# Two transformer layers on one core: implied dependencies declared away in the attention, output weights in a pool on the other side, chunk 1's operands in place of the exponentials

## The chip, the cores and the metric

The kernel runs on one core of a Trainium2 chip. The metric is the device time of one execution in microseconds (us). The engines are named as in the profile: PE (TensorE, matmuls), PEld (its weight loads), DVE (VectorE), ACT (ScalarE), POOL (GpSimd) and SP (SyncE, which here issues nearly all DMAs). Each works through its own instructions in order, and waits on semaphores that others raise.

## The reference

Two identical layers on `x` of 2048 rows by 448 columns, in float32. Each is a grouped attention with one key and one value head for 16 query heads of 28, and a gated feed-forward of width 1792, both behind a layer norm and with a residual sum:

```python
def _A_ref(x, wq, wk, wv, wo):
    q = (x @ wq).reshape(B, S, H, Dh).transpose(0, 2, 1, 3)
    k = x @ wk
    v = x @ wv
    scores = jnp.einsum("bhqd,bkd->bhqk", q, k) * (Dh ** -0.5)
    p = _softmax(scores, axis=-1)
    o = jnp.einsum("bhqk,bkd->bhqd", p, v)
    return o.transpose(0, 2, 1, 3).reshape(B, S, H * Dh) @ wo

def _B_ref(x, w_gate, w_up, w_down):
    return (_silu(x @ w_gate) * (x @ w_up)) @ w_down

x = x + _A_ref(_layernorm(x), wq, wk, wv, wo)
x = x + _B_ref(_layernorm(x), w_gate, w_up, w_down)
# and both once more
```

## The kernel before, in words

The order of instructions on each engine is the order in which the program issues them; no scheduler moves them. Semaphore waits are put in by the framework from the tiles that instructions read and write. Where an instruction needs more than one wait, wait instructions of their own stand ahead of it on its queue. A tile pool that is opened where another was closed reuses its memory, and each tile waits for the readers and writers of what lay there (`reuse_waits="tile"`).

**Precision.** Matmul operands are split into a high and a low part, so that a product of `a` and `b` is three matmuls (high by high, high by low, low by high). The 2048 rows of `x` are worked in four *chunks* of 512, whose transposed operands are a pair of tiles, `xh` and `xl`. The 448 columns are four row blocks of which the last is half full; it holds the high and the low part in one block, and a tile `xd` has those rows once more on the other half of the partitions.

**The attention's loop (`Attention.scores`).** Queries are taken in 16 groups (a chunk by four heads), keys in 16 tiles of 128. A *cycle* `m` takes two key tiles of a group, so there are 8 cycles a group and 128 a layer. In one cycle

- PE computes the scores of the first key tile for four heads (`tile_scores`, line 590): three heads go to a triple bank of PSUM, `three`, and the fourth to a single bank. Then those of the second key tile, to the other triple bank and the other single bank. The two single banks change roles from cycle to cycle.
- ACT computes four exponentials: the first single bank (line 607), the first triple (608), the second triple (611), and the second single (612). The second single was copied out of PSUM by DVE (line 610) before.
- PE multiplies the exponentials of the cycle *before* by the values (`pv`, line 639) into the single bank whose exponential line 607 has just read.
- DVE adds this product to the group's sum (line 648, or 646 for a group's first cycle). The scores of the next second key tile go to that bank, so they wait for this sum.

The exponentials have four buffers of each size, `pt` (three heads) and `pt1` (one head). After the last cycle of a group `post` sends row sums through DRAM, and a few cycles later multiplies by their reciprocals and splits the result into `onh` and `onl`. When a chunk is complete, its output projection (`outproj`, lines 575 and 579, with the weights `woh` and `wol`) stands between two cycles, three times a layer. Norm and transposition of finished chunks are dealt out over later cycles; they reach the feed-forward through DRAM (`ff.raw`).

Ahead of the loop, `q` computes queries, keys and values; ACT copies each result to a staging tile (`stage`, line 524), and SP stores it to DRAM (lines 525 and 528). `key_load` (line 383) reads the last chunk's keys back.

**The seam.** After the last cycle the feed-forward's first two units (`ff.unit(0, 0, 0)` and `(0, 0, 1)`) are issued, then the output projection of the last chunk, then `ff.rest`. A *unit* is one block of 128 of the 1792 hidden columns for one chunk: gate and up products in two halves of 11 and 10 pairs of matmuls (line 318; the two of a pair use the upper and the lower half of the array), with the down product of the unit before between and behind them. Chunk 0's operands were made during the attention. Those of chunk 1 (`parts(1, ...)`: line 278 copies on ACT, line 279 subtracts on DVE, lines 285 to 288 for the last block) are made at the start of `rest`; those of chunk 2 on POOL by the same lines, after the unit `(0, 1, 0)`; chunk 3's norm (lines 217 to 232) and transposition follow. Lines 809 and 810 add part of each chunk's down product to the residual, by a staging tile that ACT writes and POOL reads.

The pool `at` of the attention holds `woh`, `wol`, the exponentials, `tb`, `onh`, `onl` and small tiles. It is closed after the last output projection, and `stage`, `xb` (three pairs of operands) and `xd` are opened in its place.

Of the kernel before, what the change touches and what calls it, by code (L numbers as in the profile page):

```python
# [15 lines left out]
P = 128  # L16
# [39 lines left out]
def forward(  # L56
# [272 lines left out]
    class Attention:  # L329
# [223 lines left out]

        def scores(self, ff):
            next(switch)
            with tc.tile_pool(name=f"at{self.layer}", bufs=1, reuse_waits="tile") as wp:
                woh = wp.tile([P, NG, D], F32R, name="woh")
                wol = wp.tile([P, NG, D], F32R, name="wol")
                on, accs, pts = {}, {}, {}
# [23 lines left out]
                def tile_scores(n, three, one):  # L583
# [3 lines left out]
                    for z, (kp, part) in enumerate(((0, 0), (1, 0), (0, 1))):  # L587
                        for j in range(4):
# [4 lines left out]
                            )  # L593
                    pt = wp.tile([P, 3, 512], F32, name="pt", bufs=4)
                    pt1 = wp.tile([P, 512], F32, name="pt1", bufs=4)
                    pts[n] = [*(pt[:, j, :] for j in range(3)), pt1]
                    return pt, pt1

                def singles(m):
# [3 lines left out]
                def cycle(m):  # L603

                    a, b = singles(m)
                    pt, pt1 = tile_scores(2 * m, threes[0], a)
                    nc.scalar.activation(pt1, a, AF.Exp, scale=SCALE)
                    nc.scalar.activation(pt, threes[0], AF.Exp, scale=SCALE)  # L608
                    pt, pt1 = tile_scores(2 * m + 1, threes[1], b)
                    nc.vector.tensor_copy(pt1, b)  # L610
                    nc.scalar.activation(pt, threes[1], AF.Exp, scale=SCALE)  # L611
                    nc.scalar.activation(pt1, pt1, AF.Exp, scale=SCALE)

# [19 lines left out]
                def pv(m, to):  # L633
# [10 lines left out]
                    if u == 0:  # L644
                        accs[i] = halves("o2").bitcast(F32)
                        nc.vector.tensor_copy(accs[i][:, 0, :], to)
                    else:
                        nc.vector.tensor_tensor(accs[i][:, 0, :], to, accs[i][:, 0, :], ALU.add)  # L648
                    if u == NT // 2 - 1:
                        due[m + 3] = post(i)  # L650

                def post(i):
# [3 lines left out]
                    oraw, rb = out2[:, 0, :], out2[:, 1, :]  # L656
                    rs = wp.tile([P, 16], F32, name="rs", bufs=2)
                    for j in range(4):
                        nc.sync.dma_start(rs[32 * j : 32 * j + 32, :], oraw[32 * j + DH : 32 * j + DH + 1, :])

                    def rest():
                        if fine is not None:
                            under = wp.tile([P, 16], F32, name="under", bufs=2)
                            for bound, op in ((LIMIT, ALU.is_lt), (1.0 / LIMIT, ALU.is_gt)):
                                nc.vector.tensor_scalar(under, rs, bound, None, op)
                                nc.vector.tensor_tensor(fine, fine, under, ALU.mult)
# [4 lines left out]
                        if g == 0:  # L671
                            on[c] = (
                                wp.tile([P, NG, 512], F32R, name="onh"),
                                wp.tile([P, NG, 512], F32R, name="onl"),
                            )
# [68 lines left out]
                pv(last - 1, banks[6])  # L744
                self.lent = None
                next(switch)
                ff.X[0] = X0
                ff.unit(0, 0, 0)
                due.popitem()[1]()
                ff.unit(0, 0, 1)  # L750
                pos = [bank(LOW)[1] for _ in range(4)]
# [10 lines left out]
    class FeedForward:  # L762
# [61 lines left out]
        def hand_over(self, c):  # L824
# [5 lines left out]
            a.pool = self.stage  # L830
            a.X[c] = xtile(xpool if c == 0 else self.xbp)

# [91 lines left out]
        def verdict(self, last):  # L924
# [6 lines left out]
            nc.vector.tensor_reduce(whole, row[0:1, 0:P], AX.X, ALU.min)  # L931

        def rest(self, xb):
            self.stage = xb.enter_context(tc.tile_pool(name=f"stage{self.layer}", bufs=2, reuse_waits="tile"))
            self.xbp = xb.enter_context(tc.tile_pool(name=f"xb{self.layer + 1}", bufs=3, reuse_waits="tile"))
            xd = xb.enter_context(tc.tile_pool(name=f"xd{self.layer}", bufs=1, reuse_waits="tile"))
            self.xd = [xd.tile([P, 512], F32R, name=f"xd{c}") for c in range(NC)]
            dma(self.xd[0][64:128, :], self.X[0][0][0:64, 3, :])
            self.X[0] = (*self.X[0][:2], self.xd[0])
            self.parts(1, nc.scalar.copy, nc.vector.tensor_tensor)  # L940
            fs3, self.norms[3] = norm_steps(3)
            for f in fs3[:5]:
                f()
            self.fetch(2)
            self.soon.append([0, lambda: self.parts(2, nc.gpsimd.tensor_copy, nc.gpsimd.tensor_tensor)])
            self.soon.append([1, lambda: [f() for f in fs3[5:]]])
# [63 lines left out]
    for layer in range(2):  # L1010
        at.finish()
        xb.close()
        ff = FeedForward(layer)
        at.scores(ff)
        xb = ExitStack()
        ff.rest(xb)
        at = ff.nxt
# [28 lines left out]
```

## Time and profile before

| | us |
|---|---|
| median of three runs | 1998.7 (1998.66, 1998.7, 2002.25) |
| the profiled execution | 2002.23 |
| its span, first to last instruction | 2000.5 |
| PE busy | 1978.4 |
| ACT busy | 1277.5 |
| DVE busy | 785.4 |
| POOL busy | 560.4 |

The attention of layer 0 lasts from about 64 to 571 on the trace's clock, that of layer 1 from about 1054 to 1561; the rest is projections and feed-forward. Lines of a timeline read: start, duration, engine, line, operation, output and inputs, and how many were merged. A bracket has the idle time of the engine before it, and what ended it. Ends of matmuls are modelled. ACTq and PEq are the sequencers of these engines, where wait instructions run. A row that follows a stretch has its length, the busy time of PE, PEld, DVE, ACT and POOL with the number of instructions, the granted clock of PE, the share of DMA, and GB/s.

### The profile page before, as it was taken

What the parts mean: (1) busy time and instruction counts of PE and PEld (TensorE: products, weight loads), DVE (VectorE), ACT (ScalarE), POOL (GpSimd) and SP (SyncE); (2) the same over time, 40 slices, a digit from 0 to 9 for tenths busy, and PEclk for the clock granted to TensorE, in tenths of its full rate; (3) what the DMA queues carried; (4) which work ended last, traced back from release to release, by engine and by line L of the source; (5) the groups of instructions that cost most, each with busy time, mean ns of one, the idle gap of its engine ahead of it and who ended that gap; (6) DMA issues with size and microseconds to landing.
All of it is one profiled execution on the core that took longest, in us unless ns stands there. A gap on an engine that the chain in (4) does not pass through costs nothing.

```text
span 2000.5 us, 44597 instructions
## 1 busy us (share of the span) xinstructions
PE 1978.4 (99%) x18517; PEld 1337.5 (67%) x18517; DVE 785.4 (39%) x1370; ACT 1277.5 (64%) x2142; POOL 560.4 (28%) x611
## 2 busy tenths in 40 slices
PE   9999999999999999999999999999999999999998
PEld 7544545445468999999884444454454789988887
DVE  6444443443543222322464334535444332222322
ACT  4899797997953333333349998979979433333332
POOL 5222213122214233333351221122221233233320
PEclk9999999999999999999999999999999999999999
DMA  5101020021211011110031010200212100011102
GB/s 164 52 24 37 12 57 17 22 51 32 44 42 35 25 32 31 32 31 22 12 100 35 25 31 12 62 13 26 52 37 58 45 16 22 26 31 32 32 1 76
DMA packets 126343, 75.30 MB, mean 38 GB/s; under 512 B 69656, under 2 KB 109976, under 8 KB 126136
## 3 DMA queue, kind: packets, MB, share of 16 engines
q1 hardware_dynamic: 124584, 71.20, 12.9%
q8 instruction: 146, 2.39, 0.5%
q10 hardware_dynamic: 1552, 1.20, 0.2%
q14 instruction: 61, 0.50, 0.1%
HBM read 54.01 MB, written 17.83 MB: 36 GB/s over the span
## 4 chain that ended last, share of the span: by engine, by line
PE 94%; DVE 2%; POOL 1%; ACT 1%; DMA 1%; issue 0%; ACTq 0%; POOLq 0%; SPq 0%; DVEq 0%
PE bank L318 39%; PE bank L639 24%; PE three L590 17%; PE bank L590 6%; PE bank L298 4%; PE three L575 2%; PE bank L575 2%; PE bank L248 1%; POOL xl L279 0%; DMA qd<-stage 0%; ACT pt L611 0%; DVE xn L230 0%; DMA xn<-xt 0%; DMA xres<-in_A_x_dram 0%; DVE xres L579 0%
## 5 line engine op out<-in xcount | busy, mean ns | idle before, releaser
L639 PE MATMUL bank<-pt,vsb 128*32 128x512 f32 x4096 | 493.2, 598 | 0.5
L590 PE MATMUL bank<-qstack,keys 32*128 32x512 f32 x1536 | 483.8, 424 | 1.7 <-DVE xres L579 1.7
L590 PE MATMUL three<-qstack,keys 32*128 32x512 f32 x4608 | 448.8, 420 | 1.4 <-ACT stage L524 1.0
L318 PE MATMUL bank<-xh,wgh 64*128 64x512 f32 x1728 | 443.7, 391 | 4.0 <-ACT xh L278 1.4
L590 PEld LDWEIGHTS three<-qstack,keys 32*128 32x128 f32 x4608 | 258.1, 182 | 282.2 <-ACT pt L608 185.2
L611 ACT ACTIVATE pt<-three 128x1536 f32<-128x1536 f32 x256 | 383.1, 1496 | 0.0
L608 ACT ACTIVATE pt<-three 128x1536 f32<-128x1536 f32 x256 | 379.4, 1482 | 0.0
L318 PE MATMUL bank<-xh,wgl 64*128 64x512 f32 x1404 | 366.2, 391 | 0.0
L318 PE MATMUL bank<-wdh,h 64*128 64x448 f32 x1792 | 333.1, 365 | 1.2 <-ACT h L904 0.8
L318 PE MATMUL bank<-xl,wgh 64*128 64x512 f32 x1296 | 331.4, 391 | 2.6 <-POOL xl L279 2.1
L903 DVE TENSOR_TENSOR sg<-bank,sg 128x512 f32<-128x512 f32 x112 | 77.5, 692 | 511.8 <-ACT sg L902 502.6
L318 PEld LDWEIGHTS bank<-xh,wgh 64*128 64x128 f32 x1728 | 261.2, 185 | 22.5 <-POOL xh L288 2.2
L639 PEld LDWEIGHTS bank<-pt,vsb 128*32 128x32 f32 x4096 | 107.1, 109 | 249.1 <-issue 152.6
L810 POOL TENSOR_TENSOR xres<-stage,xres 128x448 f32<-128x448 f32 x108 | 127.9, 1204 | 506.0 <-ACT stage L809 506.0
L648 DVE TENSOR_TENSOR o<-bank,o 128x512 f32<-128x512 f32 x224 | 155.0, 692 | 280.5 <-PE bank L639 276.4
L610 DVE COPY pt<-bank 128x512 f32<-128x512 f32 x256 | 176.9, 691 | 205.5 <-PE bank L590 203.1
L318 PEld LDWEIGHTS bank<-wdh,h 64*128 64x128 f32 x1792 | 244.3, 185 | 14.7 <-issue 2.3
L590 PEld LDWEIGHTS bank<-qstack,keys 32*128 32x128 f32 x1536 | 243.9, 183 | 7.8 <-DVE xres L579 3.6
L677 POOL TENSOR_TENSOR o<-o 128x512 f32<-128x512 f32 x32 | 41.2, 1289 | 739.7 <-DMA o<-rd 431.6
L325 ACT COPY seen<-bank 128x1 f32<-128x1 f32 x664 | 81.4, 163 | 255.0 <-PE bank L318 249.8
L318 PEld LDWEIGHTS bank<-xh,wgl 64*128 64x128 f32 x1404 | 214.7, 185 | 13.1
L318 PE MATMUL bank<-wdl,h 64*128 64x448 f32 x896 | 218.2, 368 | 0.0
(130 smaller groups left out, 2323.5 us busy)
## 6 DMA issues: line engine op xcount, KB each, us to landing
o<-rd SPq DMA_DIRECT2D x32, 256.0 KB
qd<-stage SPq DMA_DIRECT2D x32, 224.0 KB
qraw<-qd SPq DMA_DIRECT2D x128, 56.0 KB
wdr<-in_B_w_down_dram SPq DMA_DIRECT2D x28, 224.0 KB
xt<-tb SPq DMA_DIRECT2D x96, 56.0 KB
wr<-in_B_w_gate_dram SPq DMA_DIRECT2D x28, 192.0 KB
wr<-in_B_w_up_dram SPq DMA_DIRECT2D x28, 192.0 KB
xn<-xt SPq DMA_DIRECT2D x6, 768.0 KB
```

Source lines behind the costliest of these rows:

```text
L298: nc.tensor.matmul(po, a, b, start=(i == 0), stop=(i == len(seq) - 1))
L318: nc.tensor.matmul(po, a, b, start=start, stop=stop, skip_group_check=True)
L325: nc.scalar.copy(seen[:, i : i + 1], po[:, 0:1])
L575: nc.tensor.matmul(po[:, 0:D], a[:, g, ts_], b[:, g, :], start=(g + z == 0), stop=(g == NG - 1 and z == 2))
L590: nc.tensor.matmul(three[:, j, :] if j < 3 else one, k[js, kp, ks], q[js, part, :], start=(z == 0), stop=(z == 2), tile_position=(32 * j, 0),)
L608: nc.scalar.activation(pt, threes[0], AF.Exp, scale=SCALE)
L610: nc.vector.tensor_copy(pt1, b)
L611: nc.scalar.activation(pt, threes[1], AF.Exp, scale=SCALE)
L639: nc.tensor.matmul(to[32 * j : 32 * j + 32, :], vsb[:, n % NT, :], pts[n][j], start=(y == 0), stop=(y == 1), skip_group_check=True,)
L648: nc.vector.tensor_tensor(accs[i][:, 0, :], to, accs[i][:, 0, :], ALU.add)
L810: nc.gpsimd.tensor_tensor(r, s, r, ALU.add)
L903: nc.vector.tensor_tensor(sg, pg[1], sg, ALU.mult)
```

## The change

1. The pool `at` holds only the exponentials and `tb`. The output weights, `onh`, `onl` and the small tiles are in a new pool `ow` on the right side of the memory. `at` is closed right after the last P-V, before the feed-forward's first unit.
2. The exponentials have fixed buffers, taken in turn. Between an exponential and the one that wrote its buffer two cycles before, between the copy of line 610 and that exponential, and between DVE's sum and two of its partners (the sum before, and the exponential that freed its bank), the dependency is declared away, since another wait implies it.
3. Chunk 1's operands are made ahead of the unit `(0, 0, 0)`, by a new function `begin`, in a pool that takes the place of the exponentials. Their `xd` is filled by a DMA at the start of `rest`, as chunk 0's is. Chunk 2's load (`fetch(2)`) is issued between the first two units, and its parts are made on POOL at the start of `rest`.

```diff
-        def scores(self, ff):
+        def scores(self, ff, xb):
             next(switch)
-            with tc.tile_pool(name=f"at{self.layer}", bufs=1, reuse_waits="tile") as wp:
-                woh = wp.tile([P, NG, D], F32R, name="woh")
-                wol = wp.tile([P, NG, D], F32R, name="wol")
+            inner = ExitStack()
+            with tc.tile_pool(name=f"ow{self.layer}", bufs=1, side="right", reuse_waits="tile") as ow:
+                wp = inner.enter_context(tc.tile_pool(name=f"at{self.layer}", bufs=1, reuse_waits="tile"))
+                woh = ow.tile([P, NG, D], F32R, name="woh")
+                wol = ow.tile([P, NG, D], F32R, name="wol")
...
-                    pt = wp.tile([P, 3, 512], F32, name="pt", bufs=4)
-                    pt1 = wp.tile([P, 512], F32, name="pt1", bufs=4)
+                    pt, pt1 = bufs[n % 4]
...
+                exps, sums = {}, {}
+                bufs = [
+                    (wp.tile([P, 3, 512], F32, name=f"pt{y}"), wp.tile([P, 512], F32, name=f"single{y}"))
+                    for y in range(4)
+                ]
...
-                    nc.scalar.activation(pt1, a, AF.Exp, scale=SCALE)
-                    nc.scalar.activation(pt, threes[0], AF.Exp, scale=SCALE)
+                    es = [nc.scalar.activation(pt1, a, AF.Exp, scale=SCALE)]
+                    es.append(nc.scalar.activation(pt, threes[0], AF.Exp, scale=SCALE))
                     pt, pt1 = tile_scores(2 * m + 1, threes[1], b)
-                    nc.vector.tensor_copy(pt1, b)
-                    nc.scalar.activation(pt, threes[1], AF.Exp, scale=SCALE)
-                    nc.scalar.activation(pt1, pt1, AF.Exp, scale=SCALE)
+                    copy = nc.vector.tensor_copy(pt1, b)
+                    es.append(nc.scalar.activation(pt, threes[1], AF.Exp, scale=SCALE))
+                    es.append(nc.scalar.activation(pt1, pt1, AF.Exp, scale=SCALE))
+                    exps[m] = [e.ins for e in es]
+                    for new, old in zip(exps[m], exps.get(m - 2, ())):
+                        tc.declare_no_dep(new, old, reason="P-V, which read the buffer, waited for the old one")
+                    if m > 1:
+                        tc.declare_no_dep(copy.ins, exps[m - 2][3], reason="P-V, which read it, waited for that")
...
-                        nc.vector.tensor_copy(accs[i][:, 0, :], to)
+                        f = nc.vector.tensor_copy(accs[i][:, 0, :], to)
                     else:
-                        nc.vector.tensor_tensor(accs[i][:, 0, :], to, accs[i][:, 0, :], ALU.add)
+                        f = nc.vector.tensor_tensor(accs[i][:, 0, :], to, accs[i][:, 0, :], ALU.add)
+                        if m + 1 in exps:
+                            tc.declare_no_dep(f.ins, sums[m - 1], reason="scores, ahead of this P-V, waited for the sum")
+                    sums[m] = f.ins
+                    if m + 1 in exps:
+                        tc.declare_no_dep(f.ins, exps[m + 1][0], reason="P-V waited for the bank's exponential")
...
                 pv(last - 1, banks[6])
                 self.lent = None
+                inner.close()
                 next(switch)
                 ff.X[0] = X0
+                ff.begin(xb)
                 ff.unit(0, 0, 0)
                 due.popitem()[1]()
+                ff.fetch(2)
                 ff.unit(0, 0, 1)
...
-            a.X[c] = xtile(xpool if c == 0 else self.xbp)
+            a.X[c] = xtile((xpool, self.x1p, self.xbp, self.xbp)[c])
...
+        def begin(self, xb):
+
+            self.x1p = xb.enter_context(tc.tile_pool(name=f"x1{self.layer}", bufs=1, reuse_waits="tile"))
+            self.X[1] = xtile(self.x1p)
+            halved(self.X[1], self.got.pop(1), range(4), nc.scalar.copy, nc.vector.tensor_tensor)
+
         def rest(self, xb):
...
-            self.xbp = xb.enter_context(tc.tile_pool(name=f"xb{self.layer + 1}", bufs=3, reuse_waits="tile"))
+            self.xbp = xb.enter_context(tc.tile_pool(name=f"xb{self.layer + 1}", bufs=2, reuse_waits="tile"))
...
-            dma(self.xd[0][64:128, :], self.X[0][0][0:64, 3, :])
-            self.X[0] = (*self.X[0][:2], self.xd[0])
-            self.parts(1, nc.scalar.copy, nc.vector.tensor_tensor)
+            for c in range(2):
+                dma(self.xd[c][64:128, :], self.X[c][0][0:64, 3, :])
+                self.X[c] = (*self.X[c][:2], self.xd[c])
             fs3, self.norms[3] = norm_steps(3)
             for f in fs3[:5]:
                 f()
-            self.fetch(2)
-            self.soon.append([0, lambda: self.parts(2, nc.gpsimd.tensor_copy, nc.gpsimd.tensor_tensor)])
+            self.parts(2, nc.gpsimd.tensor_copy, nc.gpsimd.tensor_tensor)
...
-        at.scores(ff)
         xb = ExitStack()
+        at.scores(ff, xb)
         ff.rest(xb)
```

The other edits of the diff put `rs`, `under`, `onh` and `onl` into `ow`.

More of the change, by code (lines that the diff above doesn't have):

```diff
@@ L656, in post @@
                     oraw, rb = out2[:, 0, :], out2[:, 1, :]
-                    rs = wp.tile([P, 16], F32, name="rs", bufs=2)
+                    rs = ow.tile([P, 16], F32, name="rs", bufs=2)
                     for j in range(4):
@@ L662, in rest @@
                         if fine is not None:
-                            under = wp.tile([P, 16], F32, name="under", bufs=2)
+                            under = ow.tile([P, 16], F32, name="under", bufs=2)
                             for bound, op in ((LIMIT, ALU.is_lt), (1.0 / LIMIT, ALU.is_gt)):
@@ L672, in rest @@
                             on[c] = (
-                                wp.tile([P, NG, 512], F32R, name="onh"),
-                                wp.tile([P, NG, 512], F32R, name="onl"),
+                                ow.tile([P, NG, 512], F32R, name="onh"),
+                                ow.tile([P, NG, 512], F32R, name="onl"),
                             )
```

## The prediction

> **What bounds the kernel now.** I read the page first, then the timeline of each engine in the attention's loop, then the places where PE sits idle, at the seams between the stages.
>
> ```profile
> span 2000.5 us, 44597 instructions
> ...
> PE 1978.4 (99%) x18517; PEld 1337.5 (67%) x18517; DVE 785.4 (39%) x1370; ACT 1277.5 (64%) x2142; POOL 560.4 (28%) x611
> ...
> L611 ACT ACTIVATE pt<-three 128x1536 f32<-128x1536 f32 x256 | 383.1, 1496 | 0.0
> ```
>
> The 99% of PE looks like a verdict, and for the feed-forward stages it is one. In the attention it isn't: there ACT's large exponential has no idle time at all before it (the 0.0 of its group), so both engines look full, and the question is which chain closes the loop. A cycle is two key tiles: scores, four exponentials, and P-V of the cycle before. The rows of ACT's line 608 in one undisturbed stretch give its length: 31 starts, 30 steps from 216.4 to 327.1, so 3.69 us a cycle.
>
> ```profile
> L608 ACT ACTIVATE pt<-three x31: 1445/1462/1530, 216.4 to 327.1; 128x1536 f32<-128x1536 f32 x31
> ```
>
> What ACT alone would need shows where it starts, before P-V and its sums have come round (ACT's timeline):
>
> ```profile
> 65.51 1.47 ACT L608 ACTIVATE pt<-three 128x1536 f32<-128x1536 f32 x1
> 66.84 1.47 ACT L611 ACTIVATE pt<-three 128x1536 f32<-128x1536 f32 x1
> 68.18 0.66 ACT L612 ACTIVATE pt<-pt 128x512 f32<-128x512 f32 x1
> 68.69 0.63 ACT L607 ACTIVATE pt<-bank 128x512 f32<-128x512 f32 x1
> 69.17 1.49 ACT L608 ACTIVATE pt<-three 128x1536 f32<-128x1536 f32 x1
> ```
>
> From start to start that is 1.33 + 1.34 + 0.51 + 0.48 = 3.66. ACT is 0.03 short of its own floor in each steady cycle. What takes the 0.03 is seen when PE, PEld and DVE are laid beside each other, later in the same loop:
>
> ```profile
> 150.18 0.39 PE L590 MATMUL bank<-qstack,keys 32*128 32x512 f32 x1
> ...
> 150.50 1.92 PE L639 MATMUL bank<-pt,vsb 128*32 128x512 f32 x16
> 150.61 0.69 DVE L610 COPY pt<-bank 128x512 f32<-128x512 f32 x1 [1.06 <-PE bank L590]
> ...
> 152.55 0.69 DVE L648 TENSOR_TENSOR o<-bank,o 128x512 f32<-128x512 f32 x1 [1.25 <-PE bank L639]
> ...
> 153.30 0.18 PEld L590 LDWEIGHTS bank<-qstack,keys 32*128 32x128 f32 x1
> ...
> 154.18 1.92 PE L639 MATMUL bank<-pt,vsb 128*32 128x512 f32 x16
> ```
>
> P-V runs from 150.50 to 152.42; the sum (line 648) starts 0.13 later and ends at 153.24; 0.06 after that PE loads weights for the single bank that the sum has just read; 0.88 later, when those scores are through, the next P-V starts: 154.18, which is 3.68 after the last. That is a closed ring through PE and DVE, and it is longer than ACT's 3.66. So in the steady loop the ring of P-V, sum and scores is the bound, by 0.02 to 0.03, and ACT comes right behind it.
>
> **The change, part by part.**
>
> *Declared dependencies.* In the program as built, ACT loses the three wait instructions that stood in each cycle, and DVE's sum loses its one: what is left is a single wait, on PE, carried by the sum itself. The price on DVE can be read above. The copy of line 610 has one wait: its scores end at 150.18 + 0.39 = 150.57 and it starts 0.04 later. The sum has a wait instruction ahead of it: 0.13. So the ring gets 0.06 to 0.09 shorter (I leave 0.03 for ends that are modelled), to 3.59 to 3.62. That is below ACT's 3.66, so ACT becomes the bound, and only 0.03 a cycle can be had, whatever else the ring gives. There are 128 cycles a layer, three of which are stretched by the output projection of a chunk; of the 127 steps 124 are regular, 248 in both layers: 248 x 0.03 = **7.4 us**. What is late next is ACT itself. Its own wait instructions cost it nothing now:
>
> ```profile
> L611 ACTq EVENT_SEMAPHORE  x252: 17/17/17, 73.1 to 1557.3; - x126
> ```
>
> They take 17 ns on its queue while a 1.33 exponential runs; line 608, which has none, is followed after the same 1.33 as line 611, which has one. The bounds of this term: nothing, if the ring has a second branch as long; and 248 x 0.065 = 16, if ACT's floor came down with the waits too.
>
> *Output weights on the other side.* This moves addresses, and with them what a buffer has to wait for. The first buffer of exponentials now lies where the attention's three staging tiles were, and the exponential of line 608 in cycle 0 of layer 0 must wait until the last of them is stored. Two rows of SP's queue show when that is, because the load of line 383 waits for the same store:
>
> ```profile
> 65.72 0.39 SPq L528 DMA_DIRECT2D kt<-stage  x1
> ...
> 68.16 0.55 SPq L383 DMA_DIRECT2D wrk<-kt  x1
> ```
>
> Line 608 would start at 68.1 instead of 65.51, and as ACT is the bound from there on, nothing hides it: a **loss of 2.6 us**, once. In layer 1 the staging tiles lie under buffers that are needed a cycle later; I put that at nothing (bound: 0.5).
>
> *Chunk 1's operands in place of exponentials.* Four copies and four subtractions move from behind the last output projection to ahead of the first feed-forward unit, where ACT and DVE have time. The seam before:
>
> ```profile
> 592.28 2.46 DVE L579 TENSOR_TENSOR xres<-bank,xres 128x448 f32<-128x448 f32 x4 [1.47 <-PE bank L575]
> ...
> 593.71 0.37 PE L575 MATMUL bank<-woh,onl 128*128 128x448 f32 x1
> 593.95 0.54 SPq L127 DMA_DIRECT2D xd<-xh  x1
> 594.11 1.66 ACT L278 CAST xh<-xn 128x512 fp32r<-128x512 f32 x3 [4.02 <-PE bank L575]
> ...
> 594.78 0.50 PE L318 MATMUL bank<-xh,wgh 64*128 64x512 f32 x2 [0.71 <-ACT xh L278]
> ...
> 597.41 0.63 DVE L217 BATCH_NORM_STATS2 stats<-xres 128x6 f32<-128x448 f32 x1
> ...
> 602.69 0.46 PE L318 MATMUL bank<-xh,wgh 64*128 64x512 f32 x2
> 602.92 0.46 PE L318 MATMUL bank<-xl,wgh 64*128 64x512 f32 x2
> ...
> 609.98 0.46 PE L318 MATMUL bank<-xh,wgh 64*128 64x512 f32 x2
> ```
>
> An undisturbed unit takes 609.98 - 602.69 = 7.29. The one before it could have begun at 594.08 and took until 602.69: 8.61, so 1.3 too long. That goes. A new wait takes part of it back: chunk 1's extra rows (xd) are now a transfer, issued behind the one of chunk 0 on SP, and both wait for the last projection. Second in the queue it is issued at about 594.7, lands 2.4 later (the store above: 65.72 to 68.16) at 597.1, and PE wants it at the eleventh pair of matmuls, 10 x 0.23 after 594.08, at 596.4: 0.7 of stall, with the queue of PE behind it. Net 0.6 to 0.7 a layer, **1.3 us** in all; bounds 0 and 2.6.
>
> *Chunk 2 earlier.* The larger part of the seam is further on. Chunk 2's parts are made on POOL, and now stand ahead of two residual sums, with their load issued between the first two units, before the output projection:
>
> ```profile
> 600.52 0.20 POOL L222 TENSOR_SCALAR rstd<-mv 128x4 f32<-128x4 f32 x1 [11.09 <-DVE mv L218]
> 600.81 1.01 POOL L223 TENSOR_TENSOR rstd<-rstd,halfn 128x4 f32<-128x4 f32 x1
> 604.21 2.36 POOL L810 TENSOR_TENSOR xres<-stage,xres 128x448 f32<-128x448 f32 x2 [2.39 <-ACT stage L809]
> 606.52 0.61 POOL L278 CAST xh<-xn 128x512 fp32r<-128x512 f32 x1
> ...
> 614.26 1.26 POOL L288 TENSOR_TENSOR xh<-xn,xd 64x512 fp32r<-64x512 f32 x1
> ...
> 623.67 2.34 POOL L810 TENSOR_TENSOR xres<-stage,xres 128x448 f32<-128x448 f32 x2 [6.03 <-ACT stage L809]
> ```
>
> Line 222 waits for statistics on DVE, which begin at 597.41 today, after chunk 1's subtractions, and then right after line 579, at 594.74: 2.67 earlier. So lines 222 and 223 end at 599.15, and the parts, which take 615.52 - 606.52 = 9.0, at 608.2 instead of 615.5. Their unit starts at 609.98 now, 609.3 then. So its waits go:
>
> ```profile
> 612.90 0.50 PE L318 MATMUL bank<-xl,wgh 64*128 64x512 f32 x2 [1.07 <-POOL xl L279]
> ...
> 615.57 0.79 PE L318 MATMUL bank<-xh,wgh 64*128 64x512 f32 x1 [0.83 <-POOL xh L288]
> ...
> 609.98:622.00 12.02, 9.51 (x69) 7.78 (x67) 3.03 (x7) 1.99 (x8) 6.76 (x10) 0.86 0.01 3
> 1600.70:1613.90 13.20, 10.98 (x68) 8.72 (x66) 3.01 (x7) 1.99 (x8) 6.75 (x10) 0.74 0.00 0
> ```
>
> The last two rows are the same unit in both layers, from its start to the next one's. Against 7.29 it loses 4.7 and 5.9: **10.6 us**. The seventh number after the span is the granted clock, 0.86 and 0.74: PE ran at half speed for part of it, and that is why the layers differ. How much of the 10.6 is clock: the parts end at 615.52, and what is left of the unit after the first 11 pairs (7.29 - 2.53) would have it end at 620.3 instead of 622.00; 1.7, and 1.2 more in layer 1, so some 4. The two residual sums that are pushed back end at 610.5 instead of 606.6; ACT needs their staging tiles again for the sums at 623.67, ahead of which POOL idled 6.03, so that costs nothing (cover gone: 4).
>
> **The sum.** The profiled execution took 2002.23, its span is 2000.5. 2002.23 - 7.4 + 2.6 - 1.3 - 10.6 = 1985.5. Of the three timed runs one took 2002.25 and two 1998.7; the profiled one stands 3.5 above their median. I take these 3.5 to be about the clock's 4: then the runs at 1998.7 lose only 7.1 in that unit, and 1998.7 - 7.4 + 2.6 - 1.3 - 7.1 = 1985.5 as well. If the 3.5 lies elsewhere, it is 1982.0. A measurement here tells 0.2% (4 us) from no change.
>
> **The rivals.** *The waits cost nothing.* Wait instructions run ahead on their queue, and the ring is closed by something as long. For it: 17 ns on ACT. Against it: the 0.13 and 0.04 on DVE. The loop stays at 3.69: 1985.5 + 7.4 = 1992.9. [...]
>
> *ACT's floor falls too.* Each start of ACT may hold a fixed share for its waits. Against it: 1.33 with and without. The ring would then be the bound at about 3.625: 248 x 0.035 = 8.7 more, 1976.8.
>
> *Half clock stays.* The granted clock falls though the waits go: 3.5 of the gain is lost, 1989. For it: the waits of PE in that unit are 1.07 and less, and a clock that falls for another reason falls again. [...]
>
> *Slower: the exponentials' new places.* If ACT's writes and PE's reads of buffers that now alternate large and small get in each other's way, each of the 512 large exponentials pays. From 0.026 each (13.2 us) all gain is gone; at 0.05 it is 25.6 and 2011. Against it: today's four buffers lie apart, and all show 1.33.
>
> **How the numbers follow.** My forecast 0.60 (its own range 1981 to 1989: the start's and the transfer's bounds, and the 3.5); waits free 0.13; floor falls 0.10; half clock 0.09; slower 0.08. The range 1976.5 to 1994 leaves out the last and the far ends. Faster by over 0.2% (under 1994.7): 0.60 + 0.10 + 0.09 and 0.07 of the second, which with the other bounds at their worst is near no change; 0.86. Same: 0.06 of it and 0.01 of the slower case, 0.07. Slower 0.07.
>
> **What would show it.** Right: steps of 3.66 between line 608's starts (now 615) instead of 3.69, and the sum 0.05 or more closer to P-V's end; cycle 0's large exponential of layer 0 starting near 68; PE waiting under 1 for chunk 1's xd; chunk 2's unit 7.3 long, clock 1.00. Wrong: cycles still 3.69 (the ring isn't what I think), POOL's parts still ending after 611, or large exponentials further apart than 1.34.

## The result, and the profile after

| | us |
|---|---|
| before, median of 7 runs | 2000.29 (1998.66 to 2002.25) |
| after, median of 7 runs | 1992.85 (1990.6 to 1995.44) |
| ratio | 0.9961 (95%: 0.9951 to 0.9971) |
| the profiled execution after, and its span | 1995.44, 1993.7 |

The change makes the kernel 7.4 us faster. The time lies inside the forecast range, near its slow end of 1994, and 7.4 above the 1985.5 that was forecast. The page of the changed kernel, its span, its engines and the two groups that the prediction named (608 is now 615):

```profile
span 1993.7 us, 43630 instructions
...
PE 1973.1 (99%) x18517; PEld 1305.8 (65%) x18517; DVE 782.7 (39%) x1370; ACT 1276.1 (64%) x2140; POOL 559.9 (28%) x611
...
L618 ACT ACTIVATE pt<-three 128x1536 f32<-128x1536 f32 x256 | 408.7, 1597 | 0.0
L615 ACT ACTIVATE pt<-three 128x1536 f32<-128x1536 f32 x256 | 405.3, 1583 | 2.6 <-DMA kt<-stage 2.6
```

Two things stand out beside the shorter span. The same exponentials last longer, 1597 ns where line 611 had 1496. And line 615 has an idle time that 608 didn't have: 2.6, ended by the store of a staging tile (`stage`).

Where the time went is read by stage. The boundaries are starts in the timelines of ACT and PE: a layer's first exponential, the large exponential of cycle 2 and of cycle 127 (line 615 or 608), the last matmul of the last output projection, the first of line 318 behind it.

| stage | before | after | difference |
|---|---|---|---|
| to the first exponential, layer 0 | 65.02 | 68.09 | +3.07 |
| from there to cycle 2 | 7.80 | 11.91 | +4.11 |
| cycles 2 to 127 | 493.61 | 492.49 | -1.12 |
| to the end of the attention | 27.27 | 27.34 | +0.07 |
| from the last projection to the feed-forward | 1.08 | 0.30 | -0.78 |
| feed-forward, next layer's projections | 460.84 | 455.89 | -4.95 |
| layer 1: to cycle 2 | 7.81 | 8.33 | +0.52 |
| layer 1: cycles 2 to 127 | 493.70 | 492.12 | -1.58 |
| layer 1: to the end of the attention | 27.29 | 27.37 | +0.08 |
| layer 1: last projection to feed-forward | 1.07 | 0.30 | -0.77 |
| layer 1: feed-forward to PE's last matmul | 408.22 | 402.54 | -5.68 |

The seams give 12.2 (the rows at -0.78, -4.95, -0.77 and -5.68), the loops 2.7 where 7.4 was forecast, and the start of the attention takes 4.1 + 0.5 where 2.6 was forecast. The first row, 3.07, lies ahead of everything that was changed. That execution ran at half clock from 16.55 to 19.97; profiled once more, the changed kernel did not, and has its first exponential at 65.29. So this is chance.

### The profile page after: what moved, and what is told of

Same layout as the page of the kernel before. It is cut to its first block, busy times and chain, and to the rows that moved or that the text cites. A ratio compares the mean times of both kernels' runs of the same rounds, so it can differ in the third digit from the quotient of the medians.

```text
span 1993.7 us, 43630 instructions
## 1 busy us (share of the span) xinstructions
PE 1973.1 (99%) x18517; PEld 1305.8 (65%) x18517; DVE 782.7 (39%) x1370; ACT 1276.1 (64%) x2140; POOL 559.9 (28%) x611
## 4 chain that ended last, share of the span: by engine, by line
PE 96%; DVE 1%; DMA 1%; ACT 1%; POOL 0%; issue 0%; ACTq 0%; SPq 0%; DVEq 0%; POOLq 0%
PE bank L318 40%; PE bank L651 25%; PE three L592 20%; PE bank L298 4%; PE bank L592 3%; PE three L577 2%; PE bank L577 2%; PE bank L248 1%; DMA wr<-in_A_wq_dram 0%; DMA qd<-stage 0%; DVE xn L230 0%; DMA xd<-xh 0%; DMA kt<-stage 0%; DVE xres L581 0%; PE bank L424 0%
## 5 line engine op out<-in xcount | busy, mean ns | idle before, releaser
L651 PE MATMUL bank<-single,vsb 128*32 128x512 f32 x1024 | 488.6, 600 | 0.0
L592 PE MATMUL bank<-qstack,keys 32*128 32x512 f32 x1536 | 470.5, 424 | 2.2 <-DVE xres L581 1.7
L592 PE MATMUL three<-qstack,keys 32*128 32x512 f32 x4608 | 461.7, 425 | 3.6 <-ACT pt L615 2.4
L592 PEld LDWEIGHTS three<-qstack,keys 32*128 32x128 f32 x4608 | 251.6, 183 | 297.0 <-ACT pt L615 187.6
L618 ACT ACTIVATE pt<-three 128x1536 f32<-128x1536 f32 x256 | 408.7, 1597 | 0.0
L615 ACT ACTIVATE pt<-three 128x1536 f32<-128x1536 f32 x256 | 405.3, 1583 | 2.6 <-DMA kt<-stage 2.6
L651 PEld LDWEIGHTS bank<-pt,vsb 128*32 128x32 f32 x3072 | 101.9, 109 | 261.2 <-issue 153.3
L617 DVE COPY single<-bank 128x512 f32<-128x512 f32 x256 | 177.0, 691 | 211.4 <-PE bank L592 205.0
L614 ACT ACTIVATE single<-bank 128x512 f32<-128x512 f32 x256 | 187.8, 734 | 64.4 <-PE bank L592 64.4
```

The source lines that it names most:

```text
L592: nc.tensor.matmul(three[:, j, :] if j < 3 else one, k[js, kp, ks], q[js, part, :], start=(z == 0), stop=(z == 2), tile_position=(32 * j, 0),)
L614: es = [nc.scalar.activation(pt1, a, AF.Exp, scale=SCALE)]
L615: es.append(nc.scalar.activation(pt, threes[0], AF.Exp, scale=SCALE))
L617: copy = nc.vector.tensor_copy(pt1, b)
L618: es.append(nc.scalar.activation(pt, threes[1], AF.Exp, scale=SCALE))
L651: nc.tensor.matmul(to[32 * j : 32 * j + 32, :], vsb[:, n % NT, :], pts[n][j], start=(y == 0), stop=(y == 1), skip_group_check=True,)
```

## The experiments

Theory A, formed from the two traces: the waits were on the ring, but ACT's true floor is not 3.66 but 3.685 a cycle, just under the ring, so little of what they cost can be collected. Theory B: they are worth the forecast 7.4, and something took it back. Theory C: the wait instructions never cost anything.

**Each half of the change alone.** The first kernel is the one before with the fixed buffers and the declarations; the second is the changed one without the declarations.

```diff
 # the kernel before, with
-pt = wp.tile([P, 3, 512], F32, name="pt", bufs=4)
-pt1 = wp.tile([P, 512], F32, name="pt1", bufs=4)
+pt, pt1 = bufs[n % 4]          # and all tc.declare_no_dep(...) of the change
 # the changed kernel, without
-tc.declare_no_dep(...)         # all four places
```

> The kernel before with the declared dependencies alone: the output weights, chunk 1's operands and chunk 2's parts stay where they were, so neither the wait at the attention's start nor the seam's gain is in it. Theory A (ScalarE's completions step by 3.685 us a cycle, and the ring of before had a mean of 3.69): the exponentials' loops shorten by 1 to 2 us a layer, so 2 to 3 us faster than before; cycles of 3.66 for some six cycles after each restart, then 3.684 to 3.686, with the exponentials' durations grown. Theory B (the waits are worth the 7.4 us of the prediction, and other edits took it back): 6 to 8 us faster. Theory C (the waits cost nothing, the chip hid them): within 1 us of before, and the loops as long as before.

> The changed kernel without the declared dependencies: new places of the exponentials, chunk 1's operands ahead, chunk 2's parts early. Theory A: the seam's 11.9 us less the start's 3 to 4.4 us: 7 to 9 us faster than before at an equal start of the kernel, so 2 to 3 us slower than the changed kernel. Theory B (the waits are worth 7.4): 7 us slower than the changed kernel, about equal to before. Theory C: equal to the changed kernel within 1 us.

Each ratio is to the kernel before, run beside that version. Declarations alone: 2001.01 against 2001.2, ratio 1.0000 (0.9991 to 1.0009). Places alone: 1995.08, 0.9963 (0.9950 to 0.9977). The whole change, run again beside later kernels, 1992.77 against 2001.68, 0.9953 (0.9939 to 0.9966):

> The changed kernel once more, beside these, so that they are compared on one chip: 0.9961 of before, as measured; its start of the kernel without the half clock of 16.5 to 20 us, so a span 3 us shorter than that profile's if that was chance.

Theory B is out. Between A and C the times don't decide: A's 2 to 3 us did not show in the first kernel's median, and would be hard to tell from nothing. The loops do: cycles 2 to 127 take 492.50 and 492.86 in the first kernel (before: 493.61 and 493.70) and 493.96 and 493.58 in the second (after: 492.49 and 492.12). So the declarations shorten the loops by 2 to 3 us, wherever they are made. (In the six profiled kernels that have all of them and the full exponentials, both loops together are 1.9 to 2.9 shorter than before.) What they leave is seen in one line's rows, between 230 and 330 us, of the kernel before, the changed one, and the first kernel:

```profile
L608 ACT ACTIVATE pt<-three x27: 1445/1460/1526, 231.1 to 327.1; 128x1536 f32<-128x1536 f32 x27
```
```profile
L615 ACT ACTIVATE pt<-three x27: 1502/1601/1607, 230.7 to 326.4; 128x1536 f32<-128x1536 f32 x27
```
```profile
L613 ACT ACTIVATE pt<-three x27: 1558/1602/1607, 230.7 to 326.5; 128x1536 f32<-128x1536 f32 x27
```

26 steps are 96.0, 95.7 and 95.8: 3.692, 3.681 and 3.685 a cycle. The median duration is the new information: 1460 before, 1601 and 1602 with the declarations, where 1445 is the shortest in these rows.

**ACT's work made smaller, in both kernels.** If ACT is the floor, a little less work on it shows what the ring alone is. These kernels leave out half of each cycle's fourth exponential.

```diff
-nc.vector.tensor_copy(pt1, b)
+nc.vector.tensor_scalar(pt1, b, 0.0, 1.0, ALU.mult, ALU.add)
-nc.scalar.activation(pt1, pt1, AF.Exp, scale=SCALE)
+nc.scalar.activation(pt1[:, 0:256], pt1[:, 0:256], AF.Exp, scale=SCALE)
```

> The kernel before with less work on ScalarE: VectorE writes ones in place of its copy of the single bank, and the fourth exponential of each cycle takes 256 of 512 columns, so that the softmax's weights of that head are not the reference's. ScalarE's work falls by some 0.23 us a cycle. Theory A (a ring P-V to sum to scores of 3.68 to 3.69 us lies just beside ScalarE's completions): the loops stay at 3.67 to 3.69, within 3 us of before. Theory C (no ring binds, the waits are hidden by ScalarE alone): cycles fall to 3.5 or less, over 30 us faster.

> The same shortening in the changed kernel, so that the softmax's weights of one head are not the reference's. Theory A: with ScalarE out of the way the ring without VectorE's wait binds, 3.61 to 3.64 a cycle, 10 to 18 us faster than the changed kernel, and 8 to 16 us more than what the shortening brings before: the waits are worth that where ScalarE isn't the floor. Theory C: it gains as much as before does.

Before stays at 2001.81 (before itself, beside it: 2001.68; ratio 1.0001, 0.9992 to 1.0010). After falls to 1979.65 (0.9890, 0.9875 to 0.9905), 13.1 under the changed kernel. The line's rows in the same stretch, shortened before and then shortened after:

```profile
L608 ACT ACTIVATE pt<-three x28: 1444/1446/1448, 229.9 to 329.5; 128x1536 f32<-128x1536 f32 x28
```
```profile
L615 ACT ACTIVATE pt<-three x27: 1444/1446/1450, 231.8 to 326.5; 128x1536 f32<-128x1536 f32 x27
```

That is 99.6 / 27 = 3.69 and 94.7 / 26 = 3.64. With ACT out of the way the kernel before doesn't move, for its ring is 3.69; the changed one drops to a ring shorter by 0.05. This is what theory A says and theory C can't: the waits did cost 0.05 a cycle, and the full exponentials hide it. The durations agree: they are at their shortest, 1446, where the ring binds and ACT waits in each cycle, and at 1601 where ACT binds.

**Which of the waits.** I tried to bring ACT down without leaving work out: VectorE copies both single banks into one tile, and one exponential of 1024 takes the place of two. It stands on the fastest version, the last of this section. The second kernel takes one declaration back in that version.

```diff
 # on the kernel with the direct operands
-es = [nc.scalar.activation(pt1, a, AF.Exp, scale=SCALE)]
+copies = [nc.vector.tensor_copy(pt1, a)]
...
-es.append(nc.scalar.activation(pt1, pt1, AF.Exp, scale=SCALE))
+es.append(nc.scalar.activation(pairs[m % 2], pairs[m % 2], AF.Exp, scale=SCALE))
 # and then also
-tc.declare_no_dep(f.ins, sums[m - 1], reason="scores, ahead of this P-V, waited for the sum")
```

In both kernels the bank is freed by a copy on DVE and not by an exponential, so the declaration of the sum on the bank's exponential has nothing to act on and is left out.

> On the kernel with the direct operands: VectorE copies both single banks of a cycle into one tile, and one exponential of 1024 columns takes the place of two of 512. By the ends of the exponentials (0.512 + 0.487 for two of 512; 1.340 for 1536, so about 0.91 for 1024) ScalarE's floor falls from 3.685 to about 3.60, below the ring of 3.63 that the shortened exponentials showed. Theory A: cycles of 3.63, 248 x 0.052 = 10 to 14 us faster than the direct operands, some 1974 to 1977. Rival: VectorE's second copy, 0.69 us a cycle, delays the sum or P-V, and the ring grows by more than 0.05: no faster, or slower.

> The same with one declaration taken back: the sum's dependency on the sum before, which puts one wait instruction ahead of each sum on VectorE. Theory A: with ScalarE out of the way the ring is back at 3.68 to 3.70, 12 to 16 us slower than without that wait. Theory C (a wait instruction costs nothing): equal within 2 us.

2019.61 (1.0088, 1.0074 to 1.0103) and 2019.36 (1.0089, 1.0075 to 1.0103). The first is the rival's case, and worse than it. DVE's timeline shows the copy queued behind other work of the attention:

```profile
274.57 0.69 DVE L662 TENSOR_TENSOR o<-bank,o 128x512 f32<-128x512 f32 x1 [1.32 <-PE bank L653]
275.18 1.44 DVE L230 TENSOR_SCALAR xn<-xres,mv,rstd 128x448 f32<-128x448 f32 x1
276.54 0.68 DVE L614 COPY pair<-bank 128x512 f32<-128x512 f32 x1
277.14 0.67 DVE L617 COPY pair<-bank 128x512 f32<-128x512 f32 x1
279.26 0.69 DVE L662 TENSOR_TENSOR o<-bank,o 128x512 f32<-128x512 f32 x1 [1.45 <-PE bank L653]
```

P-V waits for the copy of line 614, the copy stands behind a norm (230) of 1.44, and the cycle is 279.26 - 274.57 = 4.69. Cycles without such work are 3.65, and there too the forecast was off. By ends, as it counted, the exponential of 1024 takes 154.58 - 153.63 = 0.95, not 0.91:

```profile
152.19 1.44 ACT L618 ACTIVATE pt<-three 128x1536 f32<-128x1536 f32 x1
153.52 1.06 ACT L619 ACTIVATE pair<-pair 128x1024 f32<-128x1024 f32 x1
154.49 1.45 ACT L615 ACTIVATE pt<-three 128x1536 f32<-128x1536 f32 x1
```

Still the large exponentials are at their shortest here, 1.44 and 1.45, so by the sign above ACT waits, and 3.65 is the ring rather than ACT's floor.

The second kernel came out against theory A's forecast: the wait is back, and nothing is slower; cycles without other work are 3.65 as without it. Its rows say why (DVEq is DVE's sequencer; around 150 us). First this kernel, then before:

```profile
L662 DVEq EVENT_SEMAPHORE  x3: 21/21/21, 148.5 to 155.8; - x3
L662 DVE TENSOR_TENSOR o<-bank,o x3: 691/691/692, 150.3 to 157.6; 128x512 f32<-128x512 f32 x3
```
```profile
L648 DVEq EVENT_SEMAPHORE  x3: 1880/1881/1881, 146.9 to 154.3; - x3
L648 DVE TENSOR_TENSOR o<-bank,o x3: 692/692/693, 148.9 to 156.2; 128x512 f32<-128x512 f32 x3
```

Here the wait instruction is through at 148.5, 1.8 before the sum: by the program it carries DVE's own semaphore, which its 21 ns show to be raised already, and the sum itself waits for PE. Before, it lasted 1.88, from which I read that it carried DVE's and PE's, and the sum kept ACT's: the semaphore that comes last sat in the extra instruction. So theory D: a wait instruction costs something only where it carries the last semaphore. By the program, the declaration that counts is then that of the sum on the bank's exponential: without it the sum has PE's and ACT's, and PE's falls to the extra instruction. Both groups of declarations were taken back in turn, with ACT's work shortened so that the ring binds:

```diff
 # first
-tc.declare_no_dep(f.ins, exps[m + 1][0], reason="P-V waited for the bank's exponential")
 # second
-tc.declare_no_dep(new, old, reason="P-V, which read the buffer, waited for the old one")
-tc.declare_no_dep(copy.ins, exps[m - 2][3], reason="P-V, which read it, waited for that")
```

> The changed kernel with the shortened exponentials (one head's weights are not the reference's) and one declaration taken back: that of the sum on the exponential that freed its bank. The sum then has two waits, PE's and ScalarE's; PE's, which comes last, falls to a wait instruction of its own, ScalarE's to the sum. Theory D (a wait instruction costs 0.056 us only where it carries the semaphore that comes last): the sum starts 0.06 later after P-V, cycles of 3.68 to 3.70 instead of 3.633, 12 to 15 us slower than the shortened changed kernel. Rival (the ring is closed by the exponential of the single bank, not by the sum): within 3 us of it.

> The changed kernel with the shortened exponentials (one head's weights are not the reference's) and the other declarations taken back: those of the exponentials and of VectorE's copy; the sum keeps its single wait. ScalarE's wait instruction then carries PE's semaphore ahead of the single bank's exponential, which started 0.02 after it and would start 0.08 after. Theory D with a ring through the sum alone: within 3 us of the shortened changed kernel. Rival (that exponential closes the ring): 3.68 to 3.70 a cycle, 10 to 15 us slower.

1994.39 and 1980.86 (ratios to before 0.9961, 0.9948 to 0.9975, and 0.9895, 0.9880 to 0.9910), against 1979.65. The sum's rows around 150 us and line 615 in the stretch of above, for the first:

```profile
L660 DVEq EVENT_SEMAPHORE  x3: 21/21/21, 149.8 to 157.2; - x3
L660 DVE TENSOR_TENSOR o<-bank,o x3: 691/692/692, 149.9 to 157.3; 128x512 f32<-128x512 f32 x3
```
```profile
L615 ACT ACTIVATE pt<-three x27: 1444/1446/1449, 231.9 to 328.1; 128x1536 f32<-128x1536 f32 x27
```

and line 615 for the second:

```profile
L615 ACT ACTIVATE pt<-three x27: 1444/1445/1447, 231.9 to 326.6; 128x1536 f32<-128x1536 f32 x27
```

With PE's semaphore in the extra instruction, that instruction comes right ahead of the sum (149.8, 149.9), the cycle is 96.2 / 26 = 3.70, and the kernel 14.7 slower. Its loops, 494.31 and 493.88 where the shortened changed kernel has 487.23 and 486.49, are together 14.5 longer: 14.5 / 248 = 0.06 a cycle. The other declarations, which remove most of the wait instructions, give 1.2, too little to tell from nothing; so the rival, a ring through the single bank's exponential, is out. As far as these runs show, one declaration holds the whole worth of the waits. A kernel with that one alone was not run.

**Chunk 2's parts late again.**

```diff
-self.parts(2, nc.gpsimd.tensor_copy, nc.gpsimd.tensor_tensor)
+self.soon.append([0, lambda: self.parts(2, nc.gpsimd.tensor_copy, nc.gpsimd.tensor_tensor)])
```

> The changed kernel with chunk 2's parts back behind chunk 1's first unit, all else as changed. If the lateness of these parts is what made chunk 2's unit last 12.0 and 13.2 us, that unit is long again in both layers, with a window of half clock in it: 7 to 10.6 us slower than the changed kernel. Rival (chunk 1's operands ahead are what did it, since GpSimd is free earlier): less than 3 us slower, and no half clock there.

2003.26 (1.0009, 1.0000 to 1.0018), 10.5 above the changed kernel's 1992.77. The feed-forward stages are back at 462.48 and 408.56 (before 460.84 and 408.22), with half clock in both layers (mean granted clock 0.995 in its profiled execution, 0.997 in the changed kernel's). So it is the lateness of these parts, and the rival is out.

**The pool in another order.**

```diff
+tb = wp.tile([P, 4, D], F32, name="tb")
+ones = [wp.tile([P, 512], F32, name=f"single{y}") for y in range(3)]
+pt3 = wp.tile([P, 3, 512], F32, name="pt3")
+ones.append(wp.tile([P, 512], F32, name="single3"))
+bufs = [(wp.tile([P, 3, 512], F32, name=f"pt{y}"), ones[y]) for y in range(3)] + [(pt3, ones[3])]
```

> The changed kernel with the attention's pool laid out in another order: the tile of the turned rows lies first, on the staging tiles, and the exponentials' buffers behind it. Theory A: layer 0's second exponential no longer waits 2.6 us for the staging tile's stores, and the half clock of 74.6 to 78.0 us that follows that wait does not come: 4 us faster than the changed kernel (2.6 if the half clock comes all the same). Rival (the wait covers work that is late anyway, loads of keys and queries): within 1 us of the changed kernel.

1988.61 (0.9933, 0.9919 to 0.9946), 4.2 under the changed kernel's 1992.77. ACT's timeline at the start:

```profile
65.28 0.61 ACT L615 ACTIVATE single<-bank 128x512 f32<-128x512 f32 x1
65.76 1.47 ACT L616 ACTIVATE pt<-three 128x1536 f32<-128x1536 f32 x1
```

The wait is gone, and from the first exponential to cycle 2 it is 7.81 in both layers, as before the change. The loss at the start was a matter of layout alone.

**Chunk 1's doubled rows written directly.**

```diff
-self.X[1] = xtile(self.x1p)
+self.X[1] = xtile(self.x1p, self.x1p.tile([P, 512], F32R, name="xd1"))
...
-for c in range(2):
-    dma(self.xd[c][64:128, :], self.X[c][0][0:64, 3, :])
+dma(self.xd[0][64:128, :], self.X[0][0][0:64, 3, :])
```

> The other order of the attention's pool, and chunk 1's doubled rows written by ScalarE straight to their tile beside the operands instead of by a transfer behind layer's first units. The seam's 0.7 us of wait a layer goes, for one more ScalarE copy ahead of it: 1 to 1.5 us faster than the other order alone. Rival: the copy delays chunk 0's silu and the wait returns there: within 0.5 us.

This stands on the other order. 1987.39 (0.9931, 0.9917 to 0.9944), the fastest version that leaves nothing out. The step from 1988.61 is as forecast, but the intervals of the two overlap; the feed-forward stages, 455.69 and 403.29 before it, are 454.94 and 401.61.

## Why the prediction was right, and where it wasn't

**The seam: right, step by step.** The order of POOL's work in the changed kernel:

```profile
604.16 1.02 POOL L223 TENSOR_TENSOR rstd<-rstd,halfn 128x4 f32<-128x4 f32 x1
605.13 0.61 POOL L278 CAST xh<-xn 128x512 fp32r<-128x512 f32 x1
...
612.71 1.29 POOL L288 TENSOR_TENSOR xh<-xn,xd 64x512 fp32r<-64x512 f32 x1
```

The feed-forward begins at 600.13 here, 6.05 after the 594.08 that the prediction counted from. Less 6.05, line 223 ends at 599.13 (forecast 599.15) and the parts at 607.95 (forecast 608.2). The stretches of chunk 1's first unit, its second and chunk 2's:

```profile
600.13:608.05 7.92, 7.72 (x67) 6.48 (x68) 3.72 (x11) 1.36 (x7) 3.92 (x6) 1.00 0.51 130
608.05:615.34 7.29, 7.29 (x69) 6.45 (x67) 2.65 (x5) 2.87 (x10) 6.93 (x8) 1.00 0.00 1
615.34:622.63 7.29, 7.29 (x69) 6.44 (x67) 3.07 (x7) 1.99 (x8) 2.50 (x5) 1.00 0.01 2
```

Chunk 2's unit is 7.29 at clock 1.00, as forecast, and in layer 1 it is 7.29 too. Chunk 1's first unit still takes 7.92, 0.63 over: PE waits there for the transfer of `xd`, for which 0.7 was put down. Forecast for both seams 11.9, measured 12.2.

**The attention: the mechanism right, ACT's floor mis-sized.** The failed step is "That is below ACT's 3.66, so ACT becomes the bound, and only 0.03 a cycle can be had". ACT did become the bound, and the ring did become shorter by about the forecast amount (0.05, forecast 0.06 to 0.09). The sum follows P-V as the prediction's sign had it: the last matmul ends at 152.11, 0.07 ahead of the sum, where it was 0.13:

```profile
151.52 0.59 PE L651 MATMUL bank<-single,vsb 128*32 128x512 f32 x1
...
152.18 0.69 DVE L660 TENSOR_TENSOR o<-bank,o 128x512 f32<-128x512 f32 x1 [1.25 <-PE bank L651]
```

The other sign, steps of 3.66, did not come: they are 3.68, nearer to the 3.69 that was to show the prediction wrong. The 3.66 was the step between starts in the first cycle, when ACT had only just begun. ACT's timeline after one of the output projections, where it begins again after 10.58 of idle time:

```profile
352.03 1.45 ACT L615 ACTIVATE pt<-three 128x1536 f32<-128x1536 f32 x1
...
355.69 1.47 ACT L615 ACTIVATE pt<-three 128x1536 f32<-128x1536 f32 x1
...
359.34 1.50 ACT L615 ACTIVATE pt<-three 128x1536 f32<-128x1536 f32 x1
...
363.00 1.53 ACT L615 ACTIVATE pt<-three 128x1536 f32<-128x1536 f32 x1
...
366.66 1.56 ACT L615 ACTIVATE pt<-three 128x1536 f32<-128x1536 f32 x1
...
370.31 1.59 ACT L615 ACTIVATE pt<-three 128x1536 f32<-128x1536 f32 x1
...
373.99 1.60 ACT L615 ACTIVATE pt<-three 128x1536 f32<-128x1536 f32 x1
...
377.67 1.61 ACT L615 ACTIVATE pt<-three 128x1536 f32<-128x1536 f32 x1
...
381.35 1.61 ACT L615 ACTIVATE pt<-three 128x1536 f32<-128x1536 f32 x1
```

The starts step by 3.65 to 3.66 for five cycles, but each exponential ends 0.02 to 0.03 later than that: 353.48, 357.16, 360.84, 364.53, 368.22, steps of 3.68 to 3.69. At 1.60 the durations stop growing, and the starts step by 3.68 too. The ends had the floor from the first cycle on, and the prediction's own rows had it as well: 65.51 + 1.47 and 69.17 + 1.49 are 3.68 apart. With 3.685 the ring of before is longer by only 3.692 - 3.685 = 0.007, and the term would have been 248 x 0.007 = 1.7; measured 2.7, forecast 7.4.

**The start: 2.6 for the wait was right, its consequence was missed.** Line 615 waits 2.57, but layer 0 loses 4.11. Three stretches around it (the granted clock is the seventh number after the two times):

```profile
67.76:71.17 3.41, 2.34 (x23) 1.17 (x16) 1.43 (x3) 0.95 (x2) 1.91 (x2) 1.00 0.59 174
71.17:74.58 3.41, 1.44 (x20) 0.92 (x24) 1.45 (x4) 3.31 (x4) 0.00 (x0) 1.00 0.20 51
74.58:77.99 3.41, 3.41 (x28) 0.70 (x20) 0.69 (x1) 3.41 (x5) 0.99 (x2) 0.50 0.22 59
```

The wait let PE run dry (busy for 1.44 of 3.41 in the second row), and PE then ran at half clock for 3.41: 1.5 more. "What is late next" was asked of the ring, but not of the clock. In the shortened changed kernel the same wait brings no half clock, and there the way to cycle 2 grows from 7.67 to 10.33, by 2.7, the wait alone. Layer 1 lost 0.52 (0.26 when profiled again), which is the bound given beside the nothing.

**The number.** The loops gave 4.7 less than forecast, the starts took 2.0 more, the seams gave 0.3 more. The base was low as well: the sum began at 1998.7, the median of three runs, and the median of seven is 2000.29, 1.6 higher. That makes 8.0, and the median lies 7.4 above the forecast. That it still fell inside the range, 1.15 under its slow end, is owed to the range's width and not to the sum.

**The rivals.** "The waits cost nothing" would have given 1992.9, and the median is 1992.85. That agreement is chance, since the rival's mechanism is wrong: the wait instruction does cost 0.06 a cycle where it carries the last semaphore, and ACT hides it. The 2.7 that the loops did gain went again at the start and in the base. "Half clock stays" is out: there is none in the seams after (the half clocks of that trace, at 16.55 and 74.58, lie ahead of both; the rows above have 1.00). Its argument, that no wait in that unit is longer than 1.07, fails here because several stood together: 2.04 and 1.68 of idle time in the 3.41 ahead of the two half clocks of before (last section). "ACT's floor falls too" is out: the ends step by 3.68 before, where the loop begins (66.98 to 70.66), and after (the rows above). "New places of the exponentials" is out: the fastest version has other places still, and the same loops. That the profiled run's 3.5 over its median was clock is settled only in part. In 53 later runs of the kernel before, the mean time is 2000.1 at a granted clock of 0.998, 2001.4 at 0.997, 2002.4 at 0.996 and 2005.3 at 0.995 (two runs), so longer runs had less clock; but the 32 runs at 0.997 alone spread from 1999.78 to 2003.45.

## What to carry to other kernels

Read an engine's floor from the ends of its instructions in a steady stretch, not from the starts of the first ones (here 3.685, not 3.66); durations that grew from cycle to cycle (1.45 to 1.60 over six) went with an engine that was behind, and a median duration at its shortest (1446, against 1601) with one that waited. A wait instruction was worth removing where it carried the semaphore that comes last (0.06 a cycle; all the others together 1.2 us, too little to tell from nothing): look at which one the extra instruction holds, and when a ring is shortened, shorten the engine beside it too, or the gain stays hidden (2.7 us in both loops here, and 13.1 more off the kernel once ACT's work was shortened). When a pool is laid out anew, put the tile that is needed last on the memory that comes free last (4.2 us here).

## What the runs showed of the hardware

In the traces of before and after, each stretch at half clock (granted 0.50) with PE's work still ahead lasted 3.41 or 6.83 us, and began a whole number of steps of 3.413 after the trace's first record of a granted clock. In the kernel before that record is at 7.53, and the half clock began at 615.10 and 1604.97, 178 and 468 steps later; the step is read from these two, 989.87 / 290 = 3.413. In the changed kernel the record is at 6.31, and the half clock began at 16.55 and 74.58, 3 and 20 steps later. In the 3.41 just ahead of these four, PE had stood idle (by the modelled ends) for 2.04 and 1.68 us in sum before, and for 1.53 and 1.98 after; in the kernel with the dependency on the bank's exponential back, for 2.20 ahead of the half clock at 71.28. After the other stretches of this grid at full clock PE kept it in the two traces, with up to 1.03 idle before and up to 1.31 after. One case breaks this line: at the end of the kernel with the other order the clock halved at 1978.73, after PE had been busy for 2.18 of 3.41, so idle for only 1.23. Idle time alone does not draw the line, then, and what else counts stays open.

In these runs it was not always one wait, and where a stall fell on the grid made a difference. The kernel before and the same kernel with shortened exponentials have the same three waits in layer 0's seam, some 1.07, 0.60 and 0.84. Two neighbouring stretches of the grid there, first before, then shortened:

```profile
611.69:615.10 3.41, 1.37 (x7) 0.48 (x5) 0.03 (x1) 0.00 (x0) 3.21 (x4) 1.00 0.02 5
615.10:618.52 3.42, 2.95 (x16) 2.81 (x18) 1.78 (x4) 0.48 (x3) 1.92 (x5) 0.50 0.02 5
```
```profile
612.63:616.04 3.41, 2.14 (x17) 1.27 (x13) 0.69 (x1) 0.58 (x1) 3.21 (x5) 1.00 0.01 2
616.04:619.45 3.41, 2.17 (x17) 1.79 (x19) 1.69 (x4) 0.48 (x3) 2.72 (x5) 1.00 0.02 5
```

In the first, PE is busy for 1.37 in one stretch (2.04 idle) and pays with half clock in the next; in the second the border of the grid cuts the stall in two, 1.27 and 1.24 idle, and nothing follows. The start's wait shows the same: 1.98 idle in one stretch, and half clock, in the changed kernel; 1.40 and 1.42 in two, and none, in the shortened one. That goes with the size of the start's loss, for the same wait: 4.11 with the half clock, 2.7 without.

Why ACT's exponentials end 0.03 a cycle later than they start, until their durations reach 1.60, stays open.
